# Halved filter loads, half-wise tables and two-bank products at the start of an FFT-mixing and GELU kernel

## The chip, the cores and the metric

The kernel runs on one core of a Trainium2 chip. Its time is the device time of one execution in microseconds (us). Before the change the median of 3 runs was 792.26 us (791.41 to 793.5). A verdict of faster or slower is given from 2% on.

## The reference, cut to what matters

```python
# x: 8 x 3008 x 256, filt_r, filt_i: 1505 x 256, w_in: 256 x 2048, w_out: 2048 x 256, all float32
X = np.fft.rfft(x, axis=1)
y = np.fft.irfft(X * (filt_r + 1j * filt_i)[None], n=3008, axis=1)
h = y.reshape(8 * 3008, 256) @ w_in
out = (0.5 * h * (1.0 + erf(h / sqrt(2)))) @ w_out
```

## The kernel before

3008 is 47 x 64, so each Fourier transform becomes two stages of matrix products with small tables of sines (T1, T2 forward, T3, T4 inverse). The first batch can overlap with nothing, since no feed-forward work exists yet; it is a prologue that keeps all its data on the chip and turns it with TensorE transposes. The other seven batches are spread over the slots of a steady loop (`mm1`, GELU, `mm2`) and turn their data through DRAM. The prologue's stages are `c1` (first stage), `c1t` (transpose), `c2` (second stage and product with the filters), `c3` (first inverse stage), `c3t` (transpose) and `s4` (second inverse stage).

```python
    def load_filters(self, k0, k):
        nc, D = self.nc, self.D
        for t, src in enumerate((self.filt_r, self.filt_i)):
            direct = _dram(src, k0 * D, [[NA * D, 32], [D, k], [1, D]])
            mirror = _dram(src, (NA - k0) * D, [[NA * D, 32], [-D, k], [1, D]])
            for q, a in enumerate((direct, mirror, direct, mirror)):      # rows 64-127 repeat rows 0-63
                nc.gpsimd.dma_start(out=self.F[32 * q:32 * q + 32, t, k0:k0 + k, :], in_=a)

    def c2(self, p):
        nc = self.nc
        p1, p2 = (self.pp.tile([128, 512], BF16, tag=t, name=t) for t in ("p1", "p2"))
        for t, o, n in ((p1, 1, 0), (p2, 0, 1)):
            ps = self.bank("ps_c2", True)
            for i in range(2):
                k = 2 * p + i
                nc.tensor.matmul(ps[:, 256 * i:256 * i + 256], lhsT=..., rhs=..., start=True, stop=True)
            nc.vector.tensor_tensor(out=t, in0=ps, op=ALU.mult, in1=self.F[:, n, 2 * p:2 * p + 2, :]...)

    # the order of the prologue
    for k, n in ((0, 4), (4, 6), (10, 6), (16, 8)):
        m.load_filters(k, n)
    m.load_w_in()
    for u in range(16):
        m.c1(u // 2, u % 2)
        if u == 8:
            m.table_2_sin()
    m.load_x(1); m.load_w_out(0); m.load_w_out(8)                        # (three lines in the kernel)
    m.tables_inverse()                                                   # T4, T4c, T3
    for p in range(14):
        if p < 12:
            m.c1t(p)
        if 1 <= p < 13:
            m.c2(p - 1)
        if p == 4:
            nc.scalar.activation(out=warm, in_=m.p, func=AF.Gelu)        # loads the Gelu table
        if p in (3, 5, 7, 9, 11, 13):
            m.c3((p - 3) // 2)
    ...                                                                  # c3t and s4, then the steady loop
```

## Time and profile before

| stage of the kernel before | from | to | us |
|---|---|---|---|
| input, tables, `c1` | 0 | 18.4 | 18.4 |
| `c1t`, `c2`, filter products, `c3` | 18.4 | 39.6 | 21.2 |
| `c3t`, `s4` | 39.6 | 50.2 | 10.6 |
| steady loop from the first feed-forward matmul | 50.2 | 790.6 | 740.4 |

The view of busy time by stretch of time shows the same cuts. After the stretch and its length come, for each engine, the busy us and (x) the instructions, in the order that the first line gives; then the granted TensorE clock, the DMA share and the transfer rate.

```profile
core 0: us, PE busy (x) PEld busy (x) DVE busy (x) ACT busy (x) POOL busy (x), PEclk, DMA share, GB/s
0.00:18.40 18.40, 8.41 (x91) 7.83 (x92) 13.50 (x38) 10.66 (x20) 15.93 (x35) 1.00 0.83 126
18.40:39.60 21.20, 15.43 (x185) 12.42 (x182) 15.70 (x26) 13.32 (x25) 14.09 (x27) 1.00 1.12 176
39.60:50.20 10.60, 8.95 (x140) 7.26 (x141) 8.44 (x16) 8.71 (x18) 2.47 (x4) 1.00 1.20 200
50.20:790.60 740.40, 729.66 (x5406) 511.59 (x5502) 369.95 (x655) 537.79 (x920) 32.77 (x96) 1.00 0.43 107
```

In the loop TensorE is busy 729.66 of 740.40 us. The prologue is 6% of the time, and in its second stretch VectorE is the busiest engine, 15.70 of 21.20 us. The clock column says 1.00 everywhere, but for the first 18.4 us that only means that there is no clock record yet: the first one in the trace, a rise to full clock, is at 18.36 us. Up to then the 128-column transposes follow each other every 107 ns, afterwards every 56 ns, so TensorE ran at half its rate in the first stretch.

### The profile page before, as it was taken

How to read it: one execution, taken by the hardware profiler on the slowest of the kernel's cores; microseconds unless marked ns; L12 is line 12 of the kernel's file. 1: busy time of each engine (PE TensorE's matmuls, PEld its weight loads, DVE VectorE, ACT ScalarE, POOL GpSimd, SP SyncE). 2: the span in 40 equal slices, each digit the busy share in tenths (PEclk: the TensorE clock that was granted, in tenths of full speed). 3: DMA queues.
4: the chain of work that ended last, by engine and by line, in shares of the span. 5: the costliest groups of instructions: out<-in, count | busy, mean ns of one | idle time of the engine just before them, and what ended most of it. 6: DMA issues, size and time to landing. Idle time of an engine off the chain costs nothing.

```text
span 790.6 us, 14618 instructions
## 1 busy us (share of the span) xinstructions
PE 762.5 (96%) x5817; PEld 539.1 (68%) x5914; DVE 407.6 (52%) x733; ACT 570.5 (72%) x982; POOL 65.3 (8%) x161
## 2 busy tenths in 40 slices
PE   4799999999999999999999999999999999999997
PEld 4556776677676767667677676667767767666666
DVE  7784756466464645646455564546645366411011
ACT  6688965798557885588755887569865688666663
POOL 8610200011000200002000010001100000000000
PEclk9999999999999999999999999999999999999999
DMA  8994862555435553446614566154642521401111
GB/s 128 178 161 132 158 161 68 147 119 114 114 84 155 104 135 84 109 139 130 145 50 109 148 119 157 40 160 108 125 130 65 162 78 58 133 31 38 41 41 54
DMA packets 88390, 87.21 MB, mean 110 GB/s; under 512 B 6081, under 2 KB 78273, under 8 KB 88321
## 3 DMA queue, kind: packets, MB, share of 16 engines
q1 hardware_dynamic: 77760, 68.70, 30.6%
q0 software_dynamic: 10560, 17.57, 15.5%
q8 instruction: 46, 0.75, 0.4%
q14 instruction: 24, 0.19, 0.1%
HBM read 57.15 MB, written 46.66 MB: 131 GB/s over the span
## 4 chain that ended last, share of the span: by engine, by line
PE 90%; DMA 5%; DVE 2%; POOL 1%; issue 1%; ACT 0%; SPq 0%; DVEq 0%; POOLq 0%
PE ps_o L420 41%; PE ps_h L406 37%; PE ps_s L231 3%; PE ps_s L306 3%; PE ps_s L278 2%; PE ps_s L254 2%; DMA d_sb<-R 1%; DMA F<-in_filt_i_dram 1%; DMA F<-in_filt_r_dram 1%; DMA x_sb<-in_x_dram 1%; DVE d_sb L218 1%; POOL x_sb L87 1%; POOL F L95 1%; DMA R<-a_sb 1%; DMA b_sb<-R 0%
## 5 line engine op out<-in xcount | busy, mean ns | idle before, releaser
L409 ACT ACTIVATE g_sb<-ps_h 128x512 bf16<-128x512 f32 x752 | 439.4, 597 | 189.1 <-PE ps_h L406 163.5
L420 PE MATMUL ps_o<-w_out_sb,g_sb 128*128 128x256 bf16 x3008 | 449.0, 272 | 3.0
L406 PE MATMUL ps_h<-y_sb,w_in_sb 128*128 128x512 bf16 (+2 forms) x1503 | 426.6, 365 | 0.2 <-ACT y_sb L216 0.2
L420 PEld LDWEIGHTS <-g_sb 128*128 128x128 bf16 x3008 | 287.6, 98 | 133.7
L406 PEld LDWEIGHTS <-w_in_sb 128*128 128x128 bf16 x1600 | 155.1, 98 | 23.0 <-issue 0.5
L424 DVE COPY ost<-ps_o 128x512 f32<-128x512 f32 x94 | 64.4, 685 | 125.1 <-PE ps_o L420 124.6
L261 DVE TENSOR_TENSOR p<-ps_s,F 128x512 bf16<-128x512 f32 x84 | 58.1, 692 | 103.8 <-ACT p L260 97.3
L220 DVE TENSOR_SCALAR y_sb<-ps_s 128x376 bf16<-128x376 f32 x120 | 65.3, 548 | 82.0 <-PE ps_s L306 81.9
L218 DVE CAST a_sb<-ps_s 96x512 bf16<-96x512 f32 x112 | 76.3, 685 | 40.5 <-PE ps_s L231 40.4
L218 DVE CAST v_sb<-ps_s 128x512 bf16<-128x512 f32 x84 | 57.6, 687 | 12.9 <-PE ps_s L278 12.7
L306 PEld LDWEIGHTS <-d_sb 96*128 96x128 bf16 x512 | 33.8, 97 | 30.2 <-issue 2.3
L259 ACT ACTIVATE p<-ps_s 64x512 bf16<-64x512 f32 x84 | 49.9, 594 | 2.2 <-ACT g_sb L409 0.2
L260 ACT CAST p<-ps_s 64x512 bf16<-64x512 f32 x84 | 48.5, 577 | 1.0
L100 POOL COPY gate<-p 1x1 bf16<-1x1 bf16 x48 | 8.5, 176 | 480.6 <-DVE p L263 480.6
L231 PE MATMUL ps_s<-x_sb,T 94*96 94x512 bf16 x112 | 42.6, 381 | 0.5
L306 PE MATMUL ps_s<-T,d_sb 96*128 96x94 bf16 x448 | 36.3, 204 | 2.6 <-DMA d_sb<-R 1.3
L263 DVE TENSOR_TENSOR p<-p,p 128x512 bf16<-128x512 bf16 x84 | 35.7, 425 | 2.9
L87 POOL DMA_DIRECT2D x_sb<-in_x_dram x64 | 33.9, 530 | 19.0 <-issue 11.1
L262 DVE TENSOR_TENSOR p<-p,F 128x512 bf16<-128x512 bf16 x84 | 34.9, 415 | 0.0
L254 PE MATMUL ps_s<-b_sb,T 128*128 128x256 bf16 x168 | 32.1, 273 | 0.3
L278 PE MATMUL ps_s<-p,T 128*128 128x256 bf16 x168 | 32.1, 273 | 0.3
L278 PEld LDWEIGHTS <-T 128*128 128x128 bf16 x168 | 16.4, 98 | 20.1 <-DVE p L263 0.5
(84 smaller groups left out, 189.0 us busy)
## 6 DMA issues: line engine op xcount, KB each, us to landing
out_dram<-ost SPq DMA_DIRECT2D x94, 256.0 KB, 2.5
x_sb<-in_x_dram POOLq DMA_DIRECT2D x64, 188.0 KB, 3.9
R<-a_sb SPq DMA_DIRECT2D x56, 192.0 KB, 3.0
b_sb<-R SPq DMA_DIRECT2D x28, 384.0 KB, 4.4
R<-v_sb SPq DMA_DIRECT2D x42, 256.0 KB, 4.0
d_sb<-R SPq DMA_DIRECT2D x56, 192.0 KB, 4.6
w_in_sb<-in_moe_w_in_dram POOLq DMA_DIRECT2D x2, 512.0 KB, 8.6
w_out_sb<-in_moe_w_out_dram POOLq DMA_DIRECT2D x2, 512.0 KB, 10.1
```

Of the source, the lines that this page charges most:

```text
L218: self.nc.vector.tensor_copy(out=out, in_=in_)
L220: self.nc.vector.tensor_scalar(out=out, in0=in_, scalar1=scale, scalar2=None, op0=ALU.mult)
L231: nc.tensor.matmul(ps[0:96, :], lhsT=self.T1, rhs=self.st[b, "x"][:, 2 * u:2 * u + 2, :], start=True, stop=True)
L259: nc.scalar.activation(out=p2[0:64], in_=ps[64:128], func=AF.Copy, scale=-1.0)
L260: nc.scalar.copy(out=p2[64:128], in_=ps[0:64])
L261: nc.vector.tensor_tensor(out=p1, in0=ps, in1=f(0), op=ALU.mult)
L278: nc.tensor.matmul(ps[:, 256 * i:256 * i + 256], lhsT=self.T3[:, k].rearrange("p a b -> p (a b)"), rhs=w[:, 256 * i:256 * i + 256], start= ...
L306: nc.tensor.matmul(ps[:, 94 * i:94 * i + 94], lhsT=d[:, (grp % 2) * 4 + i, 128 * half:128 * half + 128], rhs=t4, start=True, stop=True)
L406: nc.tensor.matmul(ps[:, o:o + n], lhsT=self.w_in_sb[:, dc, jc * 128:jc * 128 + 128], rhs=self.ring[:, dc, off:off + n], start=(dc == 0), ...
L409: nc.scalar.activation(out=self.st["g", t][:, jc, :], in_=ps, func=AF.Gelu)
L420: nc.tensor.matmul(ps[:, tile_i % 2, :], lhsT=g[:, jc, tile_i * 128:tile_i * 128 + 128], rhs=self.w_out_sb[:, jc, :], start=(jc == 0), sto ...
L424: nc.vector.tensor_copy(out=ost, in_=ps)
```

## The change

The intent is to shorten the prologue. (Pool is the GpSimd engine; a bank is a part of PSUM, into which TensorE writes its results; an evacuation is the copy of such a result out of its bank.) (1) Each filter piece is loaded once, to partitions 0 to 63, and copied on the chip to 64 to 127: Pool copies three of the four pieces, VectorE the first. (2) The forward tables are made in two halves, so that the sines of the first half can start earlier, and the inverse table T3 is transposed before the last quarter of `c1`. (3) Transposes are bf16 and eight to a bank. (4) The product with the real and the imaginary filter is one instruction of 128 x 1024 over two PSUM banks. (5) `s4` of the first batch becomes `c4`, also over two banks. (6) Pool issues the first batch's x with no large iotas in between, so its last issue ends at 6.4 and not at 8.9 us. In the steady loop only the tiles p1 and p2 become halves of one tile.

```diff
-            for q, a in enumerate((direct, mirror, direct, mirror)):
+            for q, a in enumerate((direct, mirror)):
                 nc.gpsimd.dma_start(out=self.F[32 * q:32 * q + 32, t, k0:k0 + k, :], in_=a)
+    def dup_filters(self, eng, k0, k, ts=(0, 1)):
+        for t in ts:
+            o, i = (self.F[r:r + 64, t, k0:k0 + k, :].rearrange("p a b -> p (a b)") for r in (64, 0))
+            ...
+                eng.tensor_copy(out=o, in_=i)
 ...
+    m.table_2_angle(0, 12)
+    ...                                      # identity
+    m.table_2_angle(12, 12)
     for k, n in ((0, 4), (4, 6), (10, 6), (16, 8)):
         m.load_filters(k, n)
     m.load_w_in()
+    for k, n in ((4, 6), (10, 6), (16, 4), (20, 4)):
+        m.dup_filters(nc.gpsimd, k, n)
     for u in range(16):
-        m.c1(u // 2, u % 2)
-        if u == 8:
-            m.table_2_sin()
+        m.c1(u // 2, u % 2, False if 4 <= u < 8 or u % 2 and u > 7 else act)
+        if u == 3:
+            m.table_2_sin(0, 12)
+        if u == 7:
+            m.table_2_sin(12, 12)
+            nc.scalar.activation(out=warm, in_=m.p, func=AF.Gelu)
+            ...
+        if u == 11:
+            m.table_4()
+            for q in range(3):
+                m.table_3(q, act if q % 2 else False)
 ...
+    m.c1t(0, False)
+    m.c1t(1, act)
+    m.dup_filters(nc.vector, 0, 4)
+    for q in range(7):
+        if q < 6:
+            m.c2(2 * q)
+            if q + 2 < 6:
+                m.c1t(q + 2, act)
+            m.c2(2 * q + 1)
+        if q >= 1:
+            m.c3(q - 1)
 ...
     # in c2
-            nc.vector.tensor_tensor(out=t, in0=ps, op=ALU.mult, in1=self.F[:, n, ...])     # two of 128 x 512
+        nc.vector.tensor_tensor(out=w, in0=ps, op=ALU.mult, in1=self.F[:, :, ...])         # one of 128 x 1024
 ...
     # in the steady loop
-        p2, p1 = (self.pp.tile([128, 512], BF16, tag=t, name=t) for t in ("p2", "p1"))
+        w = self.pp.tile([128, 2, 512], BF16, tag="p12", name="p12")
+        p1, p2 = w[:, 0], w[:, 1]
```

## The prediction

> **What bounds the kernel now.** I read the page's busy shares and slices first, then the chain of waits from 0 to 70 us, then VectorE's waits and the timeline of the first 50 us. The page's slices:
>
> ```profile
> PE 762.5 (96%) x5817; PEld 539.1 (68%) x5914; DVE 407.6 (52%) x733; ACT 570.5 (72%) x982; POOL 65.3 (8%) x161
> PE   4799999999999999999999999999999999999997
> ```
>
> TensorE is full in every slice but the first two and the last. The diff leaves the loop after the first batch as it is (the same matmuls; only the product tiles p1 and p2 become halves of one tile), so what can change is the start: the stretch before the first feed-forward matmul. The timeline fixes its length and stages:
>
> ```profile
> 18.39 0.61 PE L335 MATMUL ps_c1t<-eye,at_sb 128*128 128x128 bf16 x8
> 19.87 3.08 DVE L352 TENSOR_TENSOR p<-ps_c,F 128x512 bf16<-128x512 f32 x5 [0.58 <-DMA F<-in_filt_r_dram]
> ...
> 35.26 4.28 DVE L352 TENSOR_TENSOR p<-ps_c,F 128x512 bf16<-128x512 f32 x7 [1.87 <-DMA F<-in_filt_i_dram]
> ...
> 40.61 0.23 PE L383 MATMUL ps_c3t<-eye,vt_sb 128*128 128x128 bf16 x1 [0.23 <-ACT vt_sb L370]
> ...
> 50.20 0.61 PE L406 MATMUL ps_h<-y_sb,w_in_sb 128*128 128x512 bf16 x2 [0.19 <-ACT y_sb L216]
> ```
>
> Forward transposes start at 18.4 us, products with the filters run from 19.87 to 39.55, inverse transposes start at 40.61, and the loop's first L406 starts at 50.20. The chain of waits for this stretch goes through the filters:
>
> ```profile
> 8.38 5.57 DMA x_sb<-in_x_dram
> 15.82 5.59 DMA F<-in_filt_r_dram
> 24.26 5.10 DMA F<-in_filt_i_dram
> 29.64 5.50 DMA F<-in_filt_i_dram
> ```
>
> That looks like 16 us to win. But a chain is one path; what the filters cost is what the products wait. VectorE's waits, 0 to 50 us (total, times, longest):
>
> ```profile
> DVE p L352 <- DMA F<-in_filt_i_dram: 4.1, 3, 1.9
> DVE p L352 <- DMA F<-in_filt_r_dram: 0.6, 1, 0.6
> ```
>
> Only 4.7 us. The 24 products need 24 x 0.616 us (3.08/5) = 14.8 us, and 14.8 + 4.7 is about the 19.7 us that they span. VectorE is the real floor, the filters 4.7 us on top.
>
> **What the Trainium skill says.** (1) "GPSIMD Engine Reference", section 4.1: one-input work on GpSimd is roughly line-rate. This kernel has no large Pool copy; its two iotas of 768 elements took 1.81 us together, about 1.05 ns an element plus 0.1 us. (2) "SBUF — State Buffer", section Who interferes with whom: a VectorE instruction in a 2-port mode and a GpSimd one exclude each other for the whole instruction. The trace fits: while VectorE ran its fp32 table passes (5.71 to 7.79 us), Pool's four x issues took 3.25 us, 0.81 each, against 0.53 elsewhere. (3) Same page, section Door 1: partitions 0 to 63 reach only half the DMA ports, about the rate of 32. The filters go to 32 partitions at a time and landed 3.15 MB (as bf16) from 13.95 to 35.14 us, 148 GB/s, where the weights to 128 partitions ran near 208. So half the bytes should need half the time, no more. (4) "VectorE: DVE Perf Modes", section Why PSUM operands drop a tier: a PSUM operand allows at most two elements a cycle for 16-bit data and one for fp32. The trace shows the fp32 case: 512 elements in 0.69 us.
>
> **The change, part by part.**
>
> *Filter loads.* 16 transfers instead of 32, 1.57 MB at 148 GB/s: 10.6 us after x has landed at 14.0 (x itself is limited by its DMA, a pair of pieces every 2.7 us, and can't come sooner). Filters are in at about 25 us instead of 35. Pool may have 8 transfers in flight (the ninth onward waits), so w_in is issued near 20.5 to 21.7 and only then does Pool copy. Eight copies, four of 1536 and four of 1024 elements: at 1.05 ns plus 0.1 us, 1.7 and 1.2 us, 11.6 us in all, done near 33.3. Per piece: 25.1, 28.5, 30.9, 33.3.
>
> *Tables in halves.* The old passes over 1536 elements took 1.08, 0.96, 1.76 and 1.76 us and ended at 11.37. The new first pass is a two-input one (1.0 us for 768) followed by 0.56, 0.96 and 0.96: 3.6 us a half. Starting at 5.7 as before, half one ends at 9.3, half two, after the identity, at 13.2: 1.8 us later than the whole before. In VectorE's order the four evacuations of c1's second input piece come after that (13.2 to 15.1); sine two on ScalarE runs 13.2 to 15.1, then the Gelu table load, 1.28 us, which in the old kernel lay at 24.4 where ScalarE had time. ScalarE's next evacuation (u = 8) starts at 16.5. The order on TensorE puts the inverse tables before c1's last quarter, and its banks wait for these evacuations: table 4 at 17.0, three groups of eight transposes to 18.9, each evacuated in some 1.1 us (VectorE to 20.3), c1's last group evacuated at 21.25. The forward transposes start at 21.3, not 18.3. This part costs 3.0 us.
>
> *First products.* One evacuation (1024 bf16 from PSUM, two a cycle, 0.66 us) at 22.6, then two VectorE copies of the first filter piece, some 0.4 us each: products start at 23.4, 3.5 us later than before.
>
> *Two-bank products.* 12 of 1024 elements: 1.067 + 0.083 = 1.15 us apart, 13.8 us instead of 14.8: 1.0 us gained. TensorE (some 2.3 us a pair of products: 0.86 for c2, 0.55 transposes, 0.95 for c3) and ScalarE (1.03 + 1.1) just keep pace. Products end at 37.3. Needed by them: filter pieces at 25.7, 29.2, 32.6 and 34.9, each 0.6 to 1.7 us after Pool's estimate. Narrow, but in time.
>
> *Inverse part.* Old: 40.61 to 50.20, 9.6 us, a period of 1.06 us for VectorE (0.60 + 0.46 in the chain). New: VectorE 0.60, ScalarE 0.75 a group, TensorE 8 x 0.06 + 8 x 0.055, about 0.95: 8 x 0.95 + a last evacuation of 0.85 is 8.5. Gained 1.1. The transposes write bf16 but the array passes are as many as before, so I give them nothing on TensorE; their gain is in the evacuations.
>
> *Sum.* Filter waits gone 4.7, two-bank 1.0, inverse part 1.1, against a later product start of 3.5: 3.3 us. The two-copy filter step may wait for Pool's lock: at 22.6 Pool is inside a copy of 1.7 us, and between the two copies Pool may take the lock again; 0 to 2.5 us, I take 0.8. That leaves 2.5 us; I take 2.7, since my front end stacks waits and may be a little too late. 792.3 - 2.7 = 789.6, and the first L406 at about 47.5.
>
> **Rivals.**
> *A: the chain is right* and the filters were worth much more: with a front end as early as the old one (products from 20) and no lock, products end at 33.8, the first L406 comes at 43.5 to 44, and the time is about 786. For it: x lands when it did, and the assignment of evacuations looks tuned. Against: VectorE's order, which the instruction order of the changed kernel confirms, puts all eight table passes before the evacuations.
> *B: Pool becomes the bound.* If a copy costs 1.7 ns an element and not 1.05, the copies take 2.7 and 1.85 us, end near 40, and the last two products follow: the first L406 at about 52, 794. At 2.6 cycles an element as for two-input work in the skill's GPSIMD page, 797. For it: no run here shows a Pool copy of that size and it shifts partitions. Against: the iotas' rate, and one input.
> *C: late weights and x.* Batch 1's x is now issued after Pool's copies, at 33 to 37, landing near 42; w_out near 47. x is needed from about 47 and w_out 10 us later, so C costs nothing unless B holds too.
> *D: the steady loop.* The merged product tile makes ScalarE's L259 copies wait for Pool's gate reads; these come some 10 slots earlier, so 0.
>
> **Range and chances.** A sets the low end, B the high end: 785 to 794 for 8 in 10. 2% is 15.8 us, so faster would need the first L406 at 34.4 us: with 13.8 us of products after x has landed at 14 and 8.5 us for the inverse part, I see no way; 2%. Slower needs the first L406 at 66: 1%. Within 2%: 97%.
>
> **What would show it.** Right: no product waiting for filter DMA; filters landed near 25; forward transposes near 21.3, products from 23.4 to 26 at 1.15 us spacing, inverse transposes near 38.5 to 40, the first L406 (now at its new line) near 47.5, and the rest of the span unchanged at 740.4 us. Wrong: products waiting on Pool (B), forward transposes at 18 to 19 (my front end too late, A), 2-port VectorE copies stretched far beyond 0.4 us (the lock larger than taken), or a loop of other length than 740 us (D).

## The result, and the profile after

The changed kernel takes 792.42 us (median of 4 runs, 792.4 to 793.8), against 791.84 us for the kernel before (4 runs, 791.0 to 793.5). The ratio is 1.0009, with a 95% interval of 0.9989 to 1.0029: the same. Ratios are the mean time of one kernel's fast runs over that of the other's of the same rounds, so not quite the ratio of the medians that are quoted. The profiled run of the changed kernel was its slowest, 793.8 us with a span of 792.0 us; the other three had spans of 790.6 us.

The same view of the changed kernel, busy time by stretch:

```profile
20.90:25.40 4.50, 2.69 (x32) 2.08 (x32) 3.73 (x4) 2.05 (x2) 4.50 (x4) 1.00 1.09 205
25.40:40.40 15.00, 12.54 (x148) 11.21 (x148) 13.95 (x12) 8.29 (x13) 9.70 (x15) 0.89 0.81 137
40.40:50.20 9.80, 7.95 (x142) 7.39 (x143) 7.52 (x11) 6.11 (x8) 0.00 (x0) 1.00 0.64 87
50.20:792.00 741.80, 729.81 (x5406) 511.42 (x5502) 369.09 (x654) 537.55 (x920) 32.79 (x96) 1.00 0.43 106
```

The loop begins at 50.2 us again. Before it, time has only moved: the product stage shrank to 15.0 us, but it starts at 25.4 us. Its clock was 0.89, where the kernel before had 1.00. The timeline of this part (start, duration, engine, line, operation, in square brackets the idle time just before and what ended it) answers to the one in the prediction:

```profile
19.14 10.02 POOL L99 COPY F<-F 64x1536 bf16<-64x1536 bf16 x8
21.91 0.69 DVE L227 COPY b_sb<-ps_c1t 128x1024 bf16<-128x1024 bf16 x1 [0.66 <-PE ps_c1t L339]
22.63 2.69 DVE L99 COPY F<-F 64x1024 bf16<-64x1024 bf16 x2
25.42 3.59 DVE L354 TENSOR_TENSOR p<-ps_c,F 128x1024 bf16<-128x1024 f32 x3
26.70 0.99 PE L351 MATMUL ps_c<-b_sb,T 128*128 128x256 bf16 x4 [2.57 <-DVE p L354]
29.43 1.23 DVE L354 TENSOR_TENSOR p<-ps_c,F 128x1024 bf16<-128x1024 f32 x1 [0.42 <-PE ps_c L351]
31.21 9.14 DVE L354 TENSOR_TENSOR p<-ps_c,F 128x1024 bf16<-128x1024 f32 x8 [0.55 <-PE ps_c L351]
42.04 1.50 PE L385 MATMUL ps_c3t<-eye,vt_sb 128*128 128x128 bf16 x24 [0.78 <-DVE vt_sb L227]
50.17 0.38 PE L422 MATMUL ps_h<-y_sb,w_in_sb 128*128 128x512 bf16 x1 [0.67 <-ACT y_sb L225]
```

Three things stand out. VectorE's two copies of the first filter piece took 2.69 us while Pool was inside its series of copies, which ran from 19.14 to 29.16 us. TensorE then stood still for 2.57 us, because both double banks were full and the products had not begun. And from then on the products waited twice on TensorE, 0.42 and 0.55 us, which they had not been expected to do. Why TensorE became late is seen in the stretches around its idle time:

```profile
24.00:26.70 2.70, 0.13 (x2) 0.00 (x1) 2.60 (x3) 0.75 (x1) 2.70 (x3) 1.00 0.98 196
26.70:28.50 1.80, 1.80 (x13) 1.57 (x14) 1.79 (x2) 0.00 (x0) 1.80 (x3) 0.53 0.10 18
28.50:30.50 2.00, 2.00 (x20) 1.77 (x18) 1.57 (x2) 1.24 (x2) 2.00 (x4) 0.57 0.22 23
```

After the pause TensorE ran at half its clock for 3.4 us, from 26.79 to 30.20 us by the clock records in the trace (0.53 and 0.57 are means over the stretches shown).

### The profile page after: what moved, and what is told of

It reads as the page before. It is cut to its first block, busy times and chain, and to the rows that moved or that the text cites. A ratio compares the mean times of both kernels' runs of the same rounds, so it can differ in the third digit from the quotient of the medians.

```text
span 792.0 us, 14572 instructions
## 1 busy us (share of the span) xinstructions
PE 762.1 (96%) x5817; PEld 539.9 (68%) x5914; DVE 411.2 (52%) x725; ACT 565.6 (71%) x963; POOL 64.7 (8%) x154
## 4 chain that ended last, share of the span: by engine, by line
PE 90%; DMA 3%; DVE 3%; ACT 1%; issue 1%; POOL 0%; SPq 0%; DVEq 0%; POOLq 0%
PE ps_o L436 40%; PE ps_h L422 37%; PE ps_s L240 3%; PE ps_s L313 3%; DMA d_sb<-R 3%; PE ps_s L263 2%; PE ps_s L288 2%; ACT y_sb L225 1%; PE ps_c L351 1%; PE ps_c L367 1%; DVE p L354 0%; DMA b_sb<-R 0%; DVE at_sb L227 0%; PE ps_t L216 0%; DVE F L99 0%
## 5 line engine op out<-in xcount | busy, mean ns | idle before, releaser
L229 DVE TENSOR_SCALAR y_sb<-ps_s 128x376 bf16<-128x376 f32 x112 | 61.0, 548 | 83.5 <-PE ps_s L313 83.5
L313 PEld LDWEIGHTS <-d_sb 96*128 96x128 bf16 x448 | 30.3, 97 | 29.7 <-DMA d_sb<-R 3.8
L273 DVE TENSOR_TENSOR p<-p 128x512 bf16<-128x512 bf16 x84 | 35.7, 425 | 2.9
```

The costliest lines, as they stand in the source:

```text
L229: self.nc.vector.tensor_scalar(out=out, in0=in_, scalar1=scale, scalar2=None, op0=ALU.mult)
L313: nc.tensor.matmul(ps[:, 94 * i:94 * i + 94], lhsT=d[:, (grp % 2) * 4 + i, 128 * half:128 * half + 128], rhs=t4, start=True, stop=True)
```

## The experiments

The theory after the result (theory 1): the copies of the first piece wait for Pool's lock (VectorE and Pool exclude each other, as the prediction has it), the wait starves TensorE, the pause slows its clock, and the slow clock makes the products wait again. The rivals: the VectorE copy across partitions is itself slow; the filters were never worth anything; the later front end is the whole loss; the loop got longer through the merged tile. Twelve times a kernel was run (two of them are repetitions), in three sets, each set with its own runs of the kernel before on the same chip (9 runs each; medians 791.59, 791.6 and 791.53 us). All results were correct.

### The first filter piece loaded whole, no VectorE copy

```diff
-        m.load_filters(k, n)
+        m.load_filters(k, n, full=k == 0)        # full: four transfers a table, as in the kernel before
 ...
-    m.dup_filters(nc.vector, 0, 4)
```

> The changed kernel with the first filter piece (k 0 to 3) loaded by four transfers per table as before, so that VectorE copies nothing; Pool still copies the other pieces. Theory 1 (the VectorE copies at 22.63 to 25.3 us, 2.7 us in place of 0.8, plus the slow TensorE clock after the 2.6 us hole that they make, ate the gain): first product at about 23.3 us instead of 25.42, granted clock 1.0 from 24 to 31 us, products end near 37.2, the first L422 near 47, time about 3 us under the changed kernel (789.4). Rival 2 (the copies are not on the path: TensorE or ScalarE would hold the products back anyway, or the loop got longer): products still end near 40, time unchanged within 1 us.

Measured: 790.04 us (5 runs, 789.64 to 790.92), ratio 0.9988 (0.9975 to 1.0002). The first feed-forward matmul started at 46.77 us, 3.4 us earlier than in the changed kernel, and the clock was 1.00 in every stretch between 26.7 and 34 us. The timeline has all twelve products in one piece:

```profile
21.11 9.63 POOL L99 COPY F<-F 64x1536 bf16<-64x1536 bf16 x8
23.28 13.67 DVE L354 TENSOR_TENSOR p<-ps_c,F 128x1024 bf16<-128x1024 f32 x12 [0.69 <-DMA F<-in_filt_i_dram]
```

(The 0.69 us ahead of them are put down to a filter transfer, but the matmuls of the first `c2` ran from 22.65 to 23.25 us, so it was these that ended last.) Taking the VectorE copies away removes the gap, the cold clock and the later waits at once. That shows that they come from the copies, though not yet by which way.

### TensorE kept busy through the gap

```diff
             m.c2(2 * q + 1)
+            if q == 0:
+                m.fill(24)                       # 24 matmuls 128x256 whose result nobody reads
```

> The changed kernel with 24 idle-filling matmuls of 256 columns (results unused) after the second product's matmuls, where TensorE stood idle from 24.1 to 26.7 us. The VectorE copies stay. Theory 1: the hole let the granted clock fall to 0.53; with it filled the clock stays at 1.0, the two VectorE waits of 0.4 and 0.55 us between products go, products end about 1.0 us earlier (39.3), first L422 near 49.1. Rival: the clock doesn't matter there, because VectorE is the bound; products end at 40.3 as before, first L422 at 50.2.

Measured: 792.08 us (5 runs, 791.63 to 792.19), ratio 1.0007 (0.9995 to 1.002). The clock stayed at 1.00:

```profile
22.64 2.15 DVE L99 COPY F<-F 64x1024 bf16<-64x1024 bf16 x2
24.90 13.80 DVE L354 TENSOR_TENSOR p<-ps_c,F 128x1024 bf16<-128x1024 f32 x12
26.70:28.50 1.80, 1.80 (x28) 1.71 (x26) 1.76 (x3) 0.82 (x1) 1.80 (x2) 1.00 0.04 9
```

The rise to full clock had come at 19.81 us here and at 19.96 us in the profile after, so up to the gap the two are alike. The 0.42 and 0.55 us that the products waited are gone, and the first feed-forward matmul started at 48.51 us, 1.66 us earlier. Of that, 0.5 us is another phase of the lock (2.15 instead of 2.69 us); the remaining 1.1 us is what the slow clock had cost. In the whole time nothing of it is seen: see the loop below.

### VectorE's copies without Pool's

```diff
-        m.load_filters(k, n)
+        m.load_filters(k, n, full=k > 0)         # the last three pieces are loaded whole
 ...
-    for k, n in ((4, 6), (10, 6), (16, 4), (20, 4)):
-        m.dup_filters(nc.gpsimd, k, n)
```

> The changed kernel with the two VectorE copies kept where they are, but Pool's eight copies taken away (the other pieces are loaded by four transfers). If the two copies took 1.08 and 1.68 us because Pool held the shared port, they now take about 0.42 us each and the first product starts near 23.5. If a copy from partitions 0 to 63 into 64 to 127 is slow by itself (one element a cycle), they take about 1.2 us each and the first product starts near 25. The later pieces land late here, so the end isn't of interest: products wait for the last piece, first L422 near 49 to 51.

Measured, one run: 790.15 us. The same two instructions at the same moment:

```profile
22.63 0.76 DVE L99 COPY F<-F 64x1024 bf16<-64x1024 bf16 x2
23.49 13.67 DVE L354 TENSOR_TENSOR p<-ps_c,F 128x1024 bf16<-128x1024 f32 x12
```

A copy across partitions is not slow: 0.76 us for both, and 2.69 us only beside Pool. So 1.9 us is the lock. That it is a wait, and not two copies that slow each other down evenly, shows in the single instructions of the profile after: Pool copies ended at 23.43 and 25.03 us, and each VectorE copy 0.28 us after one of them, at 23.71 and 25.32 us. The products are not held by it: twelve of them took 13.67 us here, without Pool's copies, and 13.67 us beside them in the first experiment. The expectation that the last piece would be waited for was a miss: the products ran through, and the first feed-forward matmul started at 46.97 us.

### All filters loaded whole, the rest of the change kept

```diff
-        m.load_filters(k, n)
+        m.load_filters(k, n, full=True)
 ...                                              # no copies at all
```

> The changed kernel with the filter part undone: all pieces by four transfers per table, no copies on Pool or VectorE. Theory 1 (with this front end the filter transfers were worth little, and their replacement cost what it saved): products start near 23.3, the last piece lands at 33 to 35 us, the last four products follow it (4.6 us), products end at 37.6 to 39.8, the first L422 at 47.5 to 49.7, time equal to or up to 2.5 us under the changed kernel. Rival 2 (the filter loads were the bound and their halving carried the change): first L422 3 us or more later than in the changed kernel, time 795 or more.

Measured: 790.65 us (5 runs, 790.31 to 792.47), ratio 0.9995 (0.9982 to 1.0007).

```profile
23.32 9.14 DVE L354 TENSOR_TENSOR p<-ps_c,F 128x1024 bf16<-128x1024 f32 x8 [0.69 <-DMA F<-in_filt_r_dram]
35.29 4.68 DVE L354 TENSOR_TENSOR p<-ps_c,F 128x1024 bf16<-128x1024 f32 x4 [2.83 <-DMA F<-in_filt_i_dram]
```

Now the last piece is waited for, 2.83 us, and the clock falls to 0.72 in 34 to 40 us; the first feed-forward matmul starts at 50.05 us, as in the changed kernel (50.17). This profile is of the slowest of the five runs, though; the other four had spans 1.7 to 2.2 us shorter, and two of these a mean clock of 1.0. So as written, the filter part of the change has gained nothing, and perhaps lost a little: what it saved in waits for filters it lost to the lock and to the pause behind it.

### The changed kernel once more

> The changed kernel again, unaltered, on the same chip as the next three, for a fair comparison and to see how far one profile differs from the next. Expected: 791.5 to 792.8; first L422 at 49.6 to 50.3; the stretch after it 740.4 to 742 us (the first profile had 741.8 against 740.4 of the kernel before; if that was a lasting cost of the change, it stays at 741.8, if it was chance, it comes out nearer 741).

Measured: 792.95 us (5 runs, 791.78 to 793.65), ratio 1.0014 (1.0002 to 1.0027). The two copies took 2.70 us, the products started at 25.46 us and waited 0.37 and 0.71 us, the clock was 0.50 from 27 to 30 us. The pattern repeats: the copies and their end to a few hundredths of a us, the waits to less than 0.2 us. The loop took 741.0 us (791.2 - 50.2).

### The kernel before with the filter part alone

```diff
-        m.load_filters(k, n)
+        m.load_filters(k, n, full=k == 0)        # later pieces: two transfers a table
     m.load_w_in()
+    for k, n in ((4, 6), (10, 6), (16, 4), (20, 4)):
+        m.dup_filters(nc.gpsimd, k, n)
```

> The kernel before with the filter part of the change alone: first piece by four transfers, the other three by two transfers per table and Pool's copies after w_in; old tables, old order, one-bank products, fp32 transposes. Theory 1 (the filters were worth to this kernel what its products waited for them, 4.7 us): products run from 19.9 without waits and end near 34.9, the first L406 near 45.6, time about 4.5 us under before (787). Rival A (the chain of waits is right, some 10 us): first L406 near 40. Rival B (Pool's copies come too late for products that start this early): products wait for Pool, first L406 47 or later.

Measured: 792.7 us (5 runs, 792.56 to 792.96), ratio 1.0014 (1.0001 to 1.0026). The expected 787 us was a clear miss:

```profile
24.85 9.64 POOL L100 COPY F<-F 64x1536 bf16<-64x1536 bf16 x8
26.35 0.69 DVE L357 TENSOR_TENSOR p<-ps_c,F 128x512 bf16<-128x512 f32 x1 [2.74 <-POOL F L100]
27.76 3.08 DVE L357 TENSOR_TENSOR p<-ps_c,F 128x512 bf16<-128x512 f32 x5 [0.72 <-POOL F L100]
```

In this front end Pool reached its copies only at 24.85 us, behind the issue of the weights, and the products, which started at 21.13 us (19.87 in the kernel before; here the rise to full clock came only at 20.84 us), waited 3.5 us for Pool where they had waited 4.7 us for transfers. The rival in which Pool takes the place of the filters is right here, although Pool's rate is what the prediction had taken: it is its start that is late. In these runs the halved transfers were worth something only together with the changed front end, in which Pool's copies began at 19.14 to 21.11 us.

### Table 3 transposed between the products

On top of the first experiment, the three groups of T3 transposes leave the middle of `c1`:

```diff
         if u == 11:
             m.table_4()
-            for q in range(3):
-                m.table_3(q, act if q % 2 else False)
 ...
+    m.table_3(0, act)                            # and groups 1 and 2 after c2(1) and c2(8)
```

> The run with the first piece loaded whole, and besides it the three groups of inverse-table transposes moved from the middle of c1 to after the first forward transposes (one before the first products, one after them, one later), all evacuated by ScalarE. Theory 1 (the later front end, forward transposes at 20.9 to 21.3 instead of 18.4, comes from the inverse tables in the middle of c1): forward transposes near 18.4, first product near 20.3, products end near 34.2, the first L422 near 44, time about 3 us under the run with the first piece whole (787). Rival (the front end is held by the table passes on VectorE, 5.6 to 12.9 us, so that moving the transposes changes little): forward transposes still at 20 or later, gain under 1 us.

Measured: 789.38 us (5 runs, 788.6 to 790.21), ratio 0.9972 (0.9959 to 0.9986). That is 0.3% below the kernel before, and the interval is also clear of that of the changed kernel's repetition in the same set, though it counts as the same by the 2% rule.

```profile
18.46 2.17 PE L339 MATMUL ps_c1t<-eye,at_sb 128*128 128x128 bf16 x16 [0.26 <-ACT at_sb L225]
20.43 1.06 PE L216 MATMUL ps_t<-eye,T 128*128 128x128 bf16 x8
22.13 2.36 DVE L354 TENSOR_TENSOR p<-ps_c,F 128x1024 bf16<-128x1024 f32 x2 [1.62 <-DMA F<-in_filt_r_dram]
22.81 0.61 PE L216 MATMUL ps_t<-eye,T 128*128 128x128 bf16 x8
```

The forward transposes start at 18.46 us, as in the kernel before. Of the 2.8 us won there, 1.1 us reach the first product (22.13 instead of 23.28 us), since sixteen transposes took 2.17 us where they took about 1.2 us (1.01 us for fifteen) in the changed kernel, and a T3 group of 1.06 us lies ahead of the first `c2`. (That `c2` ended at 22.10 us, so the first product waited for it and not for the transfer that the line names.) The first feed-forward matmul starts at 45.96 us. The last line shows why the transposes were slow: a T3 group took 1.06 us at 20.43 and one of the same shape 0.61 us at 22.81. The first clock record of this profile, the rise to full clock, is at 21.69 us, and up to 21.3 us the transposes follow each other every 107 ns instead of every 56. In the first experiment the rise came at 20.07 us, ahead of the forward transposes. With T3 gone from `c1`, TensorE had less to do there (busy 2.36 us of the 3.41 us up to 18.28), which may be why its clock came up later; no run shows that. So the later front end is a real loss in the changed kernel, and most of the 1.7 us that moving T3 does not win back went to TensorE's half clock (some 1.3 us, an estimate from the spacings). The first product of the control below came at 22.36 us, with the rise at 22.17. Once, for 0.25 us, a product then waited for Pool's copies: Pool is the next bound.

### Tables in one pass instead of halves

On top of the first experiment, `table_2_angle` and `table_2_sin` are called once for all 24 columns.

> The run with the first piece loaded whole, with the forward tables made in one pass of 1536 elements instead of two halves. If the halves cost VectorE time (four more instructions of some 0.16 us fixed cost), the last table pass ends about 0.6 us earlier (12.2 instead of 12.86); if starting the sines early is worth more than that, the forward transposes (20.87 us) come later by 0.5 us or more. I expect the two to cancel: forward transposes within 0.6 us of 20.9, first L422 within 0.7 us of 46.8.

Measured, one run: 789.77 us. The table passes ended at 11.95 instead of 12.86 us, the forward transposes started at 20.20 instead of about 21 us, the first product at 23.57 us (23.28) and the first feed-forward matmul at 47.28 us (46.77). So one pass was ahead by 0.7 us at the start of the transposes and behind by 0.3 us at the first product. In between lies the clock: in this profile the rise to full clock came only at 24.40 us, after the first product's matmuls, in the first experiment at 20.07 us. What the halves are worth at an equal clock is therefore not shown.

### The loop: chance of the transfers, or the merged tile?

The loop after the first feed-forward matmul took 740.4 us in the profile before and 741.8 us in the profile after, and the variants without the VectorE copies but with Pool's gained 2.9 to 4.4 us in the prologue but 1.5 to 2.5 us in the time. The only edit in the loop is the merged tile. (The prologue itself varies: the kernel before with merged tiles, below, began its loop at 49.70 us, the kernel before at 50.20.) Four kernels, in one set:

> The best version so far once more (first filter piece loaded whole, table 3 transposed between the products), as the control for the next two kernels on the same chip and to see whether its gain repeats. Both theories of the loop: 0.9972 of the kernel before again (0.996 to 0.999), first feed-forward matmul near 46.0, loop after it 741 to 742 us.

The control, the version with T3 late, gave 789.46 us (5 runs, 788.14 to 789.57), ratio 0.9968 (0.9956 to 0.9981). Its gain repeats; the first feed-forward matmul came at 45.84 us.

```diff
     # in the loop's product, on top of the control
-        w = self.pp.tile([128, 2, 512], BF16, tag="p12", name="p12")
-        p1, p2 = w[:, 0], w[:, 1]
+        p2, p1 = (self.pp.tile([128, 512], BF16, tag=t, name=t) for t in ("p2", "p1"))
```

> The same kernel, but the two halves of a product in the steady loop are separate tiles again, as in the kernel before (the first batch's product tiles move to the d_sb pool to make room). The loop after the first feed-forward matmul took some 741.0 to 741.8 us in the new kernels and 740.4 in the old one. If the merged tile costs that (wrong as rival D of the prediction has it), the loop falls to about 740.4 and the time by 1 us against the control. If the difference is only where the steady loop's transfers happen to land against TensorE, the two agree within 0.5 us and the idle time of the s4 matmuls ahead of d_sb differs at random between 1.3 and 2.7 us.

Separate tiles: 789.06 us (5 runs, 788.39 to 790.02), ratio 0.9969 (0.9956 to 0.9981), the same as the control. Its loop was 740.6 us in its profile, 1.2 us shorter than the control's, as the merged tile's cost would have it; with 1.1 us less of waits for `d_sb`; but the last kernel of this document, also with separate tiles, had 742.1 us (787.9 - 45.83). (The first batch's product tiles had to move into the pool of `d_sb`, for space.)

```diff
     # the kernel before, in its loop and in c2
-        p2, p1 = (self.pp.tile([128, 512], BF16, tag=t, name=t) for t in ("p2", "p1"))
+        w = self.pp.tile([128, 2, 512], BF16, tag="p12", name="p12")
+        p1, p2 = w[:, 0], w[:, 1]
```

> The kernel before with the one change that the diff makes inside the steady loop: p1 and p2 become halves of one tile. Merged tile to blame: 1 us slower than the kernel before (ratio 1.0013), loop 741.4. Chance of the transfers: the same within 0.5 us.

The kernel before with merged tiles: 791.83 us (5 runs, 791.33 to 792.68), ratio 1.0004 (0.9991 to 1.0018), loop 740.4 us in its profile. Neither direction shows a cost of the merged tile in the time. A cost of 1 us isn't excluded by it: the interval of this one would still hold 1.4 us.

What the profiles show in the loop are waits for transfers. The views of waits of TensorE from the loop on, and of the store queue at the end, each row with the total in us, how many times and the longest, first for the kernel before, then for the control:

```profile
PE ps_s L306 <- DMA d_sb<-R: 1.3, 3, 0.6
SPq L561 <- DMA out_dram<-ost: 1.5, 1, 1.5
```

```profile
PE ps_s L313 <- DMA d_sb<-R: 2.0, 5, 0.6
SPq L602 <- DMA out_dram<-ost: 2.4, 1, 2.4
```

The control lost 0.7 us more at `d_sb` and 0.9 us at the last output transfer, together 1.6 us against a loop longer by 1.4 us (787.6 - 45.84 = 741.8). Over all profiles the wait at `d_sb` was 0.9 to 2.7 us without order (2.7 in the profile after, 1.8 in its repetition), and the last output was waited for 1.5 us in all but the four variants with T3 late (2.2 to 2.5). Which transfers meet there, and why the last one takes longer in just those four, stays open. So does why the medians of some variants lie further from the prologue's gain than the one profile of each shows.

### One more try at the front end

> The control with separate tiles and with the first table-3 group after the first product's matmuls instead of ahead of them. In the earlier run of the control the first table-3 group took TensorE 1.06 us at 20.43 and the first product started at 22.13. If that group is what held the first product, it starts near 21.1 and the first feed-forward matmul near 45 (time 1 us below the kernel with separate tiles alone). If ScalarE, which evacuates the transposes and table 3, holds the second and third product instead, the product series gets a gap as long as what was won and the first feed-forward matmul stays at 46.

With the first T3 group behind the first `c2`, the second one round later, and separate tiles: 789.01 us (5 runs, 788.5 to 789.91), ratio 0.9971 (0.9958 to 0.9983), the same as the control. The timeline says why:

```profile
21.61 1.22 DVE L354 TENSOR_TENSOR p<-ps_c,F 128x1024 bf16<-128x1024 f32 x1 [1.10 <-DMA F<-in_filt_r_dram]
23.18 3.49 DVE L354 TENSOR_TENSOR p<-ps_c,F 128x1024 bf16<-128x1024 f32 x3 [0.35 <-PE ps_c L351]
26.87 9.14 DVE L354 TENSOR_TENSOR p<-ps_c,F 128x1024 bf16<-128x1024 f32 x8 [0.20 <-PE ps_c L351]
```

The first product came 0.75 us earlier than in the control (22.36 us), but the second and fifth then waited 0.35 and 0.20 us for TensorE, and the products ended at 36.0 us in both; the first feed-forward matmul came at 45.83 us. The outcome is that of the second expectation; the waits are put down to TensorE, where it had named ScalarE.

## Why the prediction was right, and where it was not

The time fell inside the range (792.42 us in 785 to 794, "within 2%" as given 97%), but 2.8 us above the predicted 789.6. That it fell inside is in part luck: the top of the range was there for rival B, which did not come, and no change at all, 792.3, lay inside it too. The gain of 2.7 us in the prologue did not come: the first feed-forward matmul was at 50.17 and not at 47.5 us. By the prediction's own steps:

- **Filter loads: right.** No product waited for a filter transfer, and Pool's copies took 10.02 us where 11.6 were taken, 9.63 us without the lock in the way. The last filter transfer, issued at 17.4 us, had landed by about 23 us (25 predicted). Pool's copies began at 19.14 us, earlier than thought, and were never waited for. Rival B, Pool as the bound, was wrong for this kernel.
- **Tables in halves: right.** The last pass ended at 12.86 us (13.2 predicted), the forward transposes started at 20.87 and 21.30 us (21.3), the first evacuation ended at 22.60 us (22.6). The 3.0 us that this front end costs were there; the variant with T3 late shows that about 1.1 us of them can be had back at the first product, and that TensorE's half clock at the start takes most of the rest. The prediction had no clock in this part.
- **Pool's lock: the step that failed by size.** The prediction named it, with 0 to 2.5 us, and took 0.8 us. It was 1.9 us (2.69 - 0.76). Two copies were queued behind a series of eight Pool copies, and their durations, 1.08 and 1.68 us, show that each waited, within its own duration. This was one of the prediction's own signs of being wrong, copies stretched far beyond 0.4 us.
- **"TensorE and ScalarE just keep pace": the step that failed in kind.** That holds at full clock. The lock left TensorE idle for 2.57 us, its clock went to a half, and it did not keep pace: 0.97 us of waits in the products, 1.1 us at the first feed-forward matmul as the filled gap shows. Nothing in the prediction followed an idle stretch into the clock.
- **Two-bank products: right.** Eight ran in 9.14 us, 1.14 us apart (1.15 predicted).
- **Inverse part: right in kind, a little less in size.** From the last product to the first feed-forward matmul it took 9.8 us (50.17 - 40.35) instead of 10.65 (50.20 - 39.55), a gain of 0.8 us and not 1.1.

The sum closes. The product series is 4.75 us shorter (19.68 to 14.93; 5.7 predicted), it starts 5.55 us later (19.87 to 25.42; 3.5 and 0.8 predicted), and the inverse part gains 0.83 us: 4.75 - 5.55 + 0.83 is 0.03 us, and 50.20 - 50.17 is 0.03 us. Against the predicted terms, 1.25 us were lost at the start, 0.95 us in the gaps and 0.3 us in the inverse part.

Rival A, a front end as early as before and no lock, was approached by the variant with T3 late: 45.96 us and 789.4 us where A had 43.5 to 44 and 786. Rival C cost nothing: no wait for the second batch's x or for w_out shows before the loop. Rival D's 0 is not contradicted by the times of four kernels, which can't exclude 1 us. The loop of 740 us was right for the three other runs of the changed kernel (790.6 - 50.2, if their loop also began at 50.2 us, of which there is no trace) and 1.4 us short for the profiled one.

## What to carry to other kernels

When a wait for a transfer is replaced by copies on the chip, look at which engines run beside the copies: a VectorE copy put next to a series of Pool copies waits inside its own duration, where no idle time shows it. And follow every new idle stretch of TensorE into the granted clock behind it: here a pause of 2.57 us cost another 1.1 us afterwards, enough to turn a small gain into none. Where the clock column shows 1.00 ahead of the first change of clock, check it against the spacing of equal matmuls: here TensorE ran at half its rate for the first 18 to 24 us. Loading the first piece whole, while only the later ones are copied, kept the gain, and moving the inverse tables behind the first forward transposes added a little to it in the trace, 0.8 us (46.77 to 45.96). In the time, the ratio to the kernel before was 0.997 in four sets of runs (three such kernels) and 0.999 without the move, and the intervals overlap.

## What the Trainium skill lacked or had wrong

- "SBUF — State Buffer", section Who interferes with whom: the exclusive lock is as the page has it. What it lacks is that two VectorE copies against a queue of eight Pool copies each wait once, to the end of a Pool copy, and that the wait is part of the recorded duration: 0.76 us for both alone, 2.69, 2.70 and 2.15 us beside Pool.
- "GPSIMD Engine Reference", section 4.1: "1-input is roughly line-rate" is borne out; the section has no figure beside it, and none for a copy that shifts partitions. Eight copies of bf16 from partitions 0 to 63 to 64 to 127, 10240 elements along a partition in all, took 9.63 us: 0.94 ns an element.
- "TensorE: Matmul & The Clock Gate", Part 1: the page has the clock fall after at least one idle window of about 3.4 us. Here the window need not be idle. In the fourteen profiles the clock fell to a half only at the end of stretches of 3.41 us with at most 1.41 us of matmuls (0.82 to 0.90 us in the three falls within a prologue), and never after one with 1.64 us or more; it first rose at the end of stretches with 3.12 us or more, and not after one with 2.84 us or less. With the gap filled it stayed at 1.00. The window runs freely, by the same page, and the clock records agree: they lie 3.41, 6.83 and 17.07 us apart, multiples of one window.
- No page says how a profile looks ahead of the first clock record: the clock column shows 1.00, while equal transposes were 107 ns apart before the record and 56 ns after it.
